# Attention with a top-32 mask and a mixer: softmax scales read in two transfers, and three edits where the first batch ends

## The chip, the cores and the metric

One core of a Trainium2 chip runs the kernel. The metric is the device time of one execution in microseconds (us); less is better. Each kernel is timed in several runs, and the median counts. One execution is also recorded by the hardware profiler: its span is the time from the first to the last recorded instruction, a little less than its device time.

## What is computed

Two blocks, one after the other, in float32 (the mixer's weights come as float64 and are converted on the chip):

```python
# attention: B=8 batches, H=8 heads, S=576 rows, D=64
scores = 1/sqrt(D) * q @ k.T
kth = np.partition(scores, -32, axis=-1)[..., -32:-31]     # the 32nd largest of each row
scores = np.where(scores >= kth, scores, -1e9)
attn = exp(scores - max(scores))
attn = attn / (sum(attn) + 1e-9)
x = (attn @ v), heads side by side                          # (8, 576, 512)
# mixer: U (576, 32), V (32, 576), w_ch1 (512, 2048), w_ch2 (2048, 512)
h = xt @ U @ V                    # along the rows; xt is x with rows and channels swapped
u = x + h.transpose(0, 2, 1)
out = u + maximum(u @ w_ch1, 0) @ w_ch2
```

## The kernel before, in words

**The unit of work** is a pair of heads, `g` from 0 to 31 (four pairs a batch, `NPAIR` = 4). A pair's 576 rows are cut into four tiles of 128 and a tail of 64 (`NT` = 4; tile 4 is the tail, in which the two heads share the partitions). The rows are dealt out so that tile t holds every fourth row. A step is one tile: in the first batch each pair has five steps; from pair 4 on the fourth tile and the tail are one step, so four steps a pair. `ALONE` = 20 is the number of the first batch's steps, 132 the number of all. Steps 20 to 23 are pair 4's, step 24 is tile 0 of pair 5, which the text writes (5,0).

**What a step does.** `scores` (L336) multiplies on PE into PSUM, and ACT copies to SBUF (L381; tail L401, L404). `front` (L454) finds each row's 32nd largest value on DVE: MAX8 gives the eight largest, MATCH_REPLACE8 takes them out, four rounds in all (L502, L515, L520). From pair 5 on (`blocked`) a row of 576 is first folded to 288: `fold` adds the two halves' bits on POOL (L432), `split` takes the larger of each two on DVE, out of PSUM (L434), and the smaller by subtraction on POOL (L435); the search then goes over the 288 larger ones and the best 16 of the smaller ones (L487, L485). The larger half lives in a buffer `upper`, of which there are two. A row that isn't folded needs a buffer `place` to take the search's first replacement; before the change that is a tile out of the same `upper` buffers, or `tplace` for the tail when three rows are searched together. After the search ACT scales the threshold (L546) and makes the mask's gap (L549), POOL subtracts it (L550), and ACT's exp (L439) adds each row's sum into a column of `den`, nine columns a pair (four tiles of two heads, and the tail).

**What follows a step.** The weights are turned for the product with v. From pair 6 on tiles 0 to 3 go by DVE's block transpose (`blocks`, L576), four DMA writes to DRAM (`away`, SP's queue, L582) and one read back (`PT`, ACT's queue, L591); tails and pairs 4 and 5 go by PE (`turns`, L612, L617) with ACT copies (L613, L618), pair 4's and later tails into the buffer `PTt`. `values` multiplies with v (L688, L691; tail L662) into XT (ACT L700, L669).

**The sums.** In the first batch `den` is applied where rows lie on partitions (L733). From pair 4 on `inverse` takes the reciprocal (DVE L629), turns it (L631), and writes nine rows of 128 to a DRAM tile `rd` in four DMAs (SP's queue, L635). One step later `scale` (L639) reads them back on ACT's queue, spread over the partitions: head 0's four rows to partitions 0 to 63, head 1's to 64 to 127, and the tail's likewise, four DMAs a pair in all (L645, L649), for 28 pairs. The rows of `rd` are in the order of `den`'s columns: before the change column 2t + c for tile t, head c.

**The mixing** (`mixed`, L703) runs in the background as a generator, a piece each time `fill` is called. From pair 4 on POOL multiplies XT by the scales (L719, L720), PE turns the result (L725, L738), and ACT copies it to a constant tile X (L729, L739). The tail's part of X has 64 rows from pair 4 on, 128 in the first batch, so its rows 64 to 127 are cleared once by a MEMSET, in pair 4's mixing (L736). Then come the products with U (`pT`, L750) and V (`up`, L762; in the first batch with L766, which adds X itself), copied and added on ACT and POOL (L775, L777, L778).

**The channel mixer** of a finished batch (`mlp`, L801: products L810 and L828, ACT L823 and L839, POOL L840) is cut into single products, which `fill` puts between the attention's instructions on PE, so many per step as a share of the work prescribes. The last batch's (`closing`, L889) runs at the end. The weights are converted by `next_params` (L218), one set at a time through a short pipeline: a raw load on SP's queue (L154), three ACT passes (L176, L177, L180), DVE L188, POOL L189 and L191.

**The order** on every engine's queue is the order in which the main loop (L1182 to L1321) issues things; nothing reorders it. A step n is: the end of the last step's exp; `weighted`, `scores` and `fold` of the next tile; `turn` and `back`; `scale` (L1287); a round of the search (`next(here)`); `next_params(1)` (L1289); a round; `split` of the next tile (L1300); the last round; `blocks` and `inverse` of the last step's tile; loads of a coming pair; `next_params(1)` when t is not 0 (L1318); the end of the search. One tile is special: the `split` of (5,0), in step 23, comes after the last round (`bound`, L1297 to L1305), because the three searches of that step hold both `upper` buffers as their places until then.

Of the kernel before, what the change touches and what calls it, by code (L numbers as in the profile page):

```python
# [26 lines left out]
def kernel(  # L27
# [30 lines left out]
    P = 128  # L58
# [78 lines left out]
    def half(h):  # L137
        return slice(h * D, (h + 1) * D)
# [79 lines left out]
    def next_params(n):  # L218

        while passes:  # L220
            passes.pop(0)()
        while parts:
            f64_join(*parts.pop(0))
        while raws:
            r, outs = raws.pop(0)
            if isinstance(outs, list):
                parts.append((*f64_parts(r, None), outs))
                continue
            hi, bits, low = f64_parts(r, outs)
            parts.append((hi, bits, low, [(bits, same)]))  # L230
        for _ in range(min(n, len(params))):
            srcs, outs = params.pop()
            raws.append((f64_raw(srcs), outs))
# [220 lines left out]
    def front(tiles):  # L454

        lanes = []
        for g, t in tiles:  # L460
            if t == 0:
                dens[g] = small.tile([P, 2 * NT + 1], F32, tag="den", name="den", bufs=3)
            S2, den = S2s.pop((g, t)), dens[g]
            early, pooled, gaps = ways(g, t)
            n = S2.shape[1]
            fold_of = folds.pop((g, t), None)
            for c in (1, 0) if n == 2 else (0,):
                slot = c if n == 2 or len(tiles) == 1 else 2
                lanes.append((
                    slot,  # L470
                    S2[:, c],
                    den[:, 2 * t + c : 2 * t + c + 1],
                    [a[:, c] for a in fold_of] if fold_of else None,
                    "early" if c in early else "pooled" if c in pooled else "gap" if c in gaps else "",
                ))
        W = len(lanes)
        first = small.tile([P, 3, 8], F32, tag="first", name="first", bufs=3)
        nmax = small.tile([P, 3], F32, tag="nmax", name="nmax", bufs=4)
        curs, places, ms = {}, {}, {}
        halves = [(lane[0], *lane[3]) for lane in lanes if lane[3]]  # L480
        for at_, step in ((0, 0), (0, 1), (8, 0)):
            for slot, upper, lower in halves:
                spot = upper[:, HALF + at_ : HALF + at_ + 8]
                if step:
                    nc.vector.match_replace(lower, spot, lower, NEG)  # L485
                else:
                    nc.vector.max(spot, lower)  # L487
        for slot, chunk, _, fold_of, _ in lanes:
            if fold_of:
                curs[slot] = fold_of[0]  # L490
            else:
                curs[slot] = chunk
                if slot == 2:
                    places[slot] = attn.tile([P, S], F32, tag="tplace", name="place", bufs=1)
                else:
                    places[slot] = attn.tile(
                        [P, 2, HALF + TOPK // 2], F32, tag="upper", name="upper"
                    ).rearrange("p c n -> p (c n)")[:, 0:S]
            ms[slot] = first[:, slot]
        order = [lane[0] for lane in lanes]  # L500
        for c in order:
            nc.vector.max(ms[c], curs[c])  # L502
        yield
        for i in range(1, TOPK // 8):
            if i == 1:
                nc.scalar.mul(nmax[:, 0:W], first[:, 0:W, 0], -SCALE)
                Es = {}
                for c, chunk, _, _, way in lanes:
                    if way == "early":
                        Es[c] = attn.tile([P, S], F32, tag="E", name="E")  # L510
                        weigh(chunk, Es[c], nmax[:, c : c + 1])
            for c in order:

                nxt = places.pop(c, curs[c])
                nc.vector.match_replace(nxt, ms[c], curs[c], NEG)  # L515
                curs[c] = nxt
            m8 = small.tile([P, 3, 8], F32, tag="m8", name="m8", bufs=4)
            for c in order:
                ms[c] = m8[:, c]
                nc.vector.max(ms[c], curs[c])  # L520
            yield
        for c, chunk, total, _, way in lanes:
            if way == "pooled":
                gap = attn.tile([P, S], F32, tag="E", name="E")
                nc.gpsimd.tensor_scalar(gap, chunk, ms[c][:, 7:8], NEG, ALU.is_lt, ALU.mult)
                nc.gpsimd.tensor_tensor(chunk, chunk, gap, ALU.add)  # L526
        for c, chunk, total, _, way in lanes:
            if way == "early":
                nc.vector.scalar_tensor_tensor(
                    out=chunk,  # L530
                    in0=chunk,
                    scalar=ms[c][:, 7:8],
                    in1=Es[c],
                    op0=ALU.is_ge,
                    op1=ALU.mult,
                    accum_out=total,
                )
        if t == NT:
            del qkTs[g]
        yield  # L540
        gaps = [lane for lane in lanes if lane[4] == "gap"]
        if gaps:
            slots = [lane[0] for lane in gaps]
            lo, hi = min(slots), max(slots) + 1
            least = small.tile([P, 3], F32, tag="least", name="least", bufs=3)
            nc.scalar.mul(least[:, lo:hi], m8[:, lo:hi, 7], WIDEN)  # L546
            for c, chunk, *_ in gaps:
                gap = attn.tile([P, S], F32, tag="E", name="E")
                nc.scalar.activation(gap, chunk, AF.Relu, bias=least[:, c : c + 1], scale=-WIDEN)  # L549
                nc.gpsimd.tensor_tensor(chunk, chunk, gap, ALU.subtract)  # L550
            yield
        rest = [lane for lane in lanes if lane[4] != "early"]
        if len(gaps) > 1:
            c, chunk, total, *_ = rest.pop(0)
            weigh(chunk, chunk, nmax[:, c : c + 1], total)
            yield
        for c, chunk, total, *_ in rest:
            weigh(chunk, chunk, nmax[:, c : c + 1], total)
        if t == NT and g != NPAIR - 1:
            nc.scalar.activation(den, den, AF.Identity, bias=eps)  # L560
        yield
# [77 lines left out]
    def scale(g):  # L639

        rd = scales.pop(g)
        sc = attn.tile([P, S], F32, tag="scale", name="scale", bufs=1)
        scales[g] = sc
        for h in range(2):
            nc.scalar.dma_start(  # L645
                sc[half(h), 0:MAIN].rearrange("p (t n) -> p t n", t=NT),
                rd[0 : 2 * NT].rearrange("(t h) n -> h t n", h=2)[h : h + 1].to_broadcast([D, NT, P]),
            )
            nc.scalar.dma_start(  # L649
                sc[half(h), MAIN:S], rd[2 * NT : 2 * NT + 1, half(h)].to_broadcast([D, TAIL])  # L650
            )

    def values(g, t):

# [48 lines left out]
    def mixed(g, wait, lag=0):  # L703
# [26 lines left out]
        if g < NPAIR:  # L730
            X4 = X4.rearrange("p t (h d) -> p t h d", h=2)
            den4 = den[:, 0 : 2 * NT].rearrange("p (t h) -> p t h ()", h=2)
            nc.gpsimd.tensor_tensor(X4, X4, den4.to_broadcast([P, NT, 2, D]), ALU.mult)  # L733
        else:
            if g == NPAIR:
                nc.gpsimd.memset(X[TAIL:P, NT, :], 0.0)  # L736
            tp = ps_t.tile([P, P], F32, tag="tp", name="tp")
            nc.tensor.transpose(tp[0:TAIL], uT[:, at(NT)], ident)  # L738
            nc.scalar.copy(X[0:TAIL, NT, :], tp[0:TAIL])  # L739
# [20 lines left out]
        for chunks, (lo, hi) in zip(PARTS, SPAN):  # L760
# [15 lines left out]
            else:  # L776
                nc.scalar.copy(sc[:, lo:hi], up[:, 0 : hi - lo])  # L777
                nc.gpsimd.tensor_tensor(uT[:, lo:hi], uT[:, lo:hi], sc[:, lo:hi], ALU.add)  # L778
            yield
        if gi == NPAIR - 1:  # L780
            fillers.append(closing(b) if b == B - 1 else mlp(b))

# [370 lines left out]
    def tiles(n):  # L1153

        return steps[n] if 0 <= n < STEPS else []
# [26 lines left out]
    for n in range(STEPS + 2):  # L1182
# [103 lines left out]
        if n < STEPS and n - 2 >= ALONE and len(tiles(n - 2)) > 1:  # L1286
            scale(steps[n - 2][0][0])  # L1287
        next(here, None)
        next_params(1)  # L1289
        fill()  # L1290
        if n >= STEPS:
            if n == STEPS:
# [1 line left out]
                scale(NP - 1)  # L1294
            weighted(n - 2)
        next(here, None)
        bound = tiles(n + 1)[:1] == [(NPAIR + 1, 0)]  # L1297
        if not bound:
            for tile_ in tiles(n + 1):
                split(*tile_)  # L1300
        fill()
        next(here, None)
        if bound:
            for tile_ in tiles(n + 1):
                split(*tile_)  # L1305
        for tile_ in tiles(n - 1):
            if shared(*tile_):
                blocks(*tile_)
# [5 lines left out]
                coming = loading(g + 2) if g + 2 < NP else iter(())  # L1314
            next(coming, None)
        next(ready, None)
        if t != 0:
            next_params(1)  # L1318
        next(here, None)
        fill()  # L1320
# [36 lines left out]
```

## Time and profile before

| | |
|---|---|
| median of 3 runs | 1684.32 us (1682.92 to 1688.65) |
| the profiled execution | 1686.09 us, span 1684.0 us |
| mean granted clock of TensorE | 0.963 |
| busy, share of the span | PE 93%, DVE 92%, ACT 59%, POOL 59% |
| DMA packets | 295631, 189.42 MB, mean 112 GB/s |
| reads of the scales | 56 of 128 KB (L645) and 56 of 16 KB (L649), on ACT's queue |

PE is TensorE (PEld its weight loads, which lie beside the products), DVE VectorE, ACT ScalarE, POOL GpSimd, SP SyncE. "ACTq" and "SPq" are an engine's issuing of DMAs. L12 is line 12 of the kernel. In a list of waits each row says which engine and line waited for which, then how long in sum, how often, and the longest. In a timeline a row is the start, the duration, the engine, the line and the operation with its shape, and in brackets how long the engine had been idle before it and who released it. The granted clock is the share of TensorE's full speed that the chip's throttle allowed.

### The profile page before, as it was taken

The numbers are of one execution on the slowest core, as the hardware profiler recorded it, in microseconds if no ns is written. First come the engines' busy times: TensorE is split into PE (matmuls) and PEld (weight loads), VectorE is DVE, ScalarE is ACT, GpSimd is POOL, SyncE is SP. The second block draws the span as 40 slices with busy tenths as digits, with TensorE's granted clock in tenths as the row PEclk, the third lists the DMA queues.
The fourth block names the chain that finished last, engine by engine and source line by source line (L and its number), as shares of the span: only waits on it lengthen the run. The fifth ranks groups of instructions, "written<-read, shape, count | busy, mean of one in ns | idle before, by whom it ended". The sixth has DMA issues, their size and how long they took to land.

```text
span 1684.0 us, 30301 instructions
## 1 busy us (share of the span) xinstructions
PE 1569.8 (93%) x9638; PEld 1189.6 (71%) x9638; DVE 1546.0 (92%) x4393; ACT 992.5 (59%) x2475; POOL 1000.3 (59%) x853
## 2 busy tenths in 40 slices
PE   4667798999899999999999999999999999999999
PEld 2444466777577886778777787778777787778776
DVE  7999998899999999999999999999999999995452
ACT  4888777665655656556655566556655566564320
POOL 4778668666656565655656565655656565653620
PEclk7787798999999999999999999999999999999999
DMA  3323232254555555555455555554555555543001
GB/s 87 96 74 96 61 94 73 56 128 130 136 128 131 134 151 131 127 138 131 124 128 139 127 139 135 132 139 124 133 128 132 133 140 136 132 126 109 10 1 29
DMA packets 295631, 189.42 MB, mean 112 GB/s; under 512 B 178768, under 2 KB 279984, under 8 KB 295472
## 3 DMA queue, kind: packets, MB, share of 16 engines
q1 hardware_dynamic: 259728, 117.62, 30.2%
q10 hardware_dynamic: 35744, 69.88, 13.6%
q8 instruction: 76, 1.25, 0.3%
q14 instruction: 83, 0.68, 0.1%
HBM read 116.49 MB, written 70.91 MB: 111 GB/s over the span
## 4 chain that ended last, share of the span: by engine, by line
DVE 47%; PE 33%; DMA 8%; SPq 4%; issue 3%; ACT 2%; POOL 1%; ACTq 0%; DVEq 0%; POOLq 0%
DVE m L520 13%; DVE upper L515 11%; PE mm L828 9%; PE mm L810 8%; DVE y L576 5%; DVE first L502 4%; DVE upper L487 4%; DMA ld<-in_k_dram 3%; PE sc L336 3%; DVE place L515 3%; PE mm L904 3%; DVE lower L485 3%; PE O L691 2%; DMA PT<-away 2%; PE sc L904 2%
## 5 line engine op out<-in xcount | busy, mean ns | idle before, releaser
L810 PE MATMUL mm<-uT,w 128*128 128x320 f32 (+1 forms) x1792 | 468.1, 413 | 14.5 <-ACT hT L823 14.1
L550 POOL TENSOR_TENSOR Ssb<-Ssb,E 128x576 f32<-128x576 f32 x243 | 340.0, 1419 | 208.8 <-ACT E L549 208.4
L828 PE MATMUL mm<-hT,w 128*128 128x320 f32 (+1 forms) x1792 | 462.8, 408 | 0.0
L810 PEld LDWEIGHTS mm<-uT,w 128*128 128x128 f32 x1792 | 336.1, 192 | 120.2 <-ACT hT L823 23.3
L828 PEld LDWEIGHTS mm<-hT,w 128*128 128x128 f32 x1792 | 332.5, 190 | 93.6 <-issue 11.0
L520 DVE MAX8 m<-upper 128x8 f32<-128x304 f32 (+1 forms) x780 | 377.8, 539 | 0.7
L515 DVE MATCH_REPLACE8 upper<-m,upper 128x304 f32<-128x304 f32 (+1 forms) x520 | 266.8, 534 | 0.0
L435 POOL TENSOR_TENSOR lower<-lower,upper 128x576 uint32<-128x576 uint32 x108 | 152.9, 1416 | 162.0 <-DVE upper L434 161.7
L439 ACT ACTIVATE Ssb<-Ssb,nmax 128x576 f32<-128x576 f32 x258 | 201.8, 783 | 32.9 <-POOL Ssb L526 9.9
L432 POOL TENSOR_TENSOR lower<-Ssb 128x576 uint32<-128x576 uint32 x108 | 152.4, 1411 | 93.3 <-ACT Ssb L381 48.7
L487 DVE MAX8 upper<-lower 128x8 f32<-128x288 f32 x432 | 176.8, 461 | 15.9 <-POOL lower L435 15.8
L336 PE MATMUL sc<-qkT 64*128 64x288 f32 (+1 forms) x1056 | 179.6, 462 | 11.0 <-ACT Ssb L390 7.8
L549 ACT ACTIVATE E<-Ssb,least 128x576 f32<-128x576 f32 x243 | 176.3, 769 | 4.2
L381 ACT COPY Ssb<-sc 128x576 f32<-128x576 f32 x216 | 127.8, 644 | 61.6 <-PE sc L336 61.6
L576 DVE STREAM_TRANSPOSE y<-Ssb 128x512 f32<-128x512 f32 (+1 forms) x312 | 157.7, 581 | 0.3 <-ACT Ssb L439 0.2
L823 ACT ACTIVATE hT<-mm 128x320 f32<-128x320 f32 (+1 forms) x224 | 91.3, 410 | 102.7 <-PE mm L810 97.9
L691 PE MATMUL O<-PT,va 128*64 128x128 f32 x2048 | 144.5, 285 | 0.0
L336 PEld LDWEIGHTS sc<-qkT 64*128 64x128 f32 (+1 forms) x1056 | 96.0, 197 | 52.0 <-issue 17.4
L691 PEld LDWEIGHTS O<-PT,va 128*64 128x64 f32 x2048 | 113.3, 140 | 16.4 <-issue 2.0
L515 DVE MATCH_REPLACE8 upper<-first,upper 128x304 f32<-128x304 f32 x216 | 100.4, 487 | 0.0
L485 DVE MATCH_REPLACE8 lower<-upper,lower 128x288 f32<-128x288 f32 x216 | 96.3, 465 | 0.0
L434 DVE TENSOR_TENSOR upper<-sc,Ssb 128x576 f32<-128x576 f32 x108 | 83.3, 772 | 11.5 <-ACT Stail L401 11.5
(264 smaller groups left out, 2246.9 us busy)
## 6 DMA issues: line engine op xcount, KB each, us to landing
away<-y SPq DMA_DIRECT2D x416, 144.0 KB
PT<-away ACTq DMA_DIRECT2D x104, 576.0 KB
raw<-in_moe_w_ch_dram SPq DMA_DIRECT2D x32, 512.0 KB
va<-in_v_dram SPq DMA_DIRECT2D x64, 128.0 KB
out_dram<-ob SPq DMA_DIRECT2D x59, 128.0 KB
scale<-rd ACTq DMA_DIRECT2D x56, 128.0 KB
ld<-in_q_dram SPq DMA_DIRECT2D x108, 64.0 KB
ld<-in_k_dram SPq DMA_DIRECT2D x108, 64.0 KB
```

The source lines that it names most:

```text
L336: nc.tensor.matmul(out, lhsT=qkT[half(h), 0, cols(t)], rhs=qkT[half(h), 1, lo:hi], start=True, stop=True,)
L435: nc.gpsimd.tensor_tensor(bottom, bottom, top.bitcast(U32), ALU.subtract)
L439: nc.scalar.activation(E, chunk, AF.Exp, bias=nmax, scale=SCALE, accum_out=total)
L487: nc.vector.max(spot, lower)
L515: nc.vector.match_replace(nxt, ms[c], curs[c], NEG)
L520: nc.vector.max(ms[c], curs[c])
L549: nc.scalar.activation(gap, chunk, AF.Relu, bias=least[:, c : c + 1], scale=-WIDEN)
L550: nc.gpsimd.tensor_tensor(chunk, chunk, gap, ALU.subtract)
L576: nc.vector.transpose(y[:, :, i * NT : i * NT + c].rearrange("p r c j -> p c r j"), E2[:, a : a + c * P].rearrange("p (c r j) -> p c r j", ...
L691: nc.tensor.matmul(O[half(h)], lhsT=va[:, h, j, :], rhs=PT[:, NT * h + j], start=False, stop=(j == NT - 1),)
L810: nc.tensor.matmul(ph[:, 0:w], lhsT=first_layer(cc, f), rhs=uT[:, cc, lo:hi], start=(cc == 0), stop=(cc == NC - 1),)
L828: nc.tensor.matmul(po[:, 0:w], lhsT=w2[:, f, c * P : (c + 1) * P], rhs=hTs[f][:, 0:w], start=(f == 0), stop=(f == NF - 1),)
```

## The change

Four edits.

1. *Scales.* From pair 4 on the columns of `den` are ordered by head: column 4c + t. The scale rows of one head are then 2 KB in a row in DRAM, and `scale` reads all 128 partitions' main part in one DMA (source 2 heads, each repeated for 64 partitions, 512 values) and the tail's in another (2 x 64 repeats x 64 values). Two DMAs a pair in the place of four, on the same queue at the same place.
2. *The sixth pair's first fold.* The searches of step 23 take their places from the `scale` and `PTt` buffers, which hold nothing yet, so the `split` of (5,0) comes where that of every other tile does, ahead of the last round.
3. *Parameters.* Step 23 leaves out its first `next_params(1)`; step 24 gets one at its end. From step 25 on as many have been done as before.
4. *X's rows.* The MEMSET of rows 64 to 127 moves from pair 4's mixing to the end of pair 3's.

```diff
@@ front
             for c in (1, 0) if n == 2 else (0,):
                 slot = c if n == 2 or len(tiles) == 1 else 2
+                spot = NT * c + t if g >= NPAIR and t < NT else 2 * t + c
                 lanes.append((
                     slot,
                     S2[:, c],
-                    den[:, 2 * t + c : 2 * t + c + 1],
+                    den[:, spot : spot + 1],
...
                 if slot == 2:
                     places[slot] = attn.tile([P, S], F32, tag="tplace", name="place", bufs=1)
+                elif (g, t) == (NPAIR, NT):
+                    places[slot] = attn.tile([P, S], F32, tag="scale", name="place", bufs=1) if slot else (
+                        attn.tile([P, NT + 1, P], F32, tag="PTt", name="place", bufs=1)
+                    ).rearrange("p c n -> p (c n)")[:, 0:S]
                 else:
@@ scale
-        for h in range(2):
-            nc.scalar.dma_start(
-                sc[half(h), 0:MAIN].rearrange("p (t n) -> p t n", t=NT),
-                rd[0 : 2 * NT].rearrange("(t h) n -> h t n", h=2)[h : h + 1].to_broadcast([D, NT, P]),
-            )
-            nc.scalar.dma_start(
-                sc[half(h), MAIN:S], rd[2 * NT : 2 * NT + 1, half(h)].to_broadcast([D, TAIL])
-            )
+        full = rd[0 : 2 * NT].rearrange("(h t) n -> h () (t n)", h=2)
+        nc.scalar.dma_start(sc[:, 0:MAIN], full.to_broadcast([2, D, MAIN]))
+        ends = rd[2 * NT : 2 * NT + 1].rearrange("o (h n) -> (o h) () n", h=2)
+        nc.scalar.dma_start(sc[:, MAIN:S], ends.to_broadcast([2, D, TAIL]))
@@ mixed
-            if g == NPAIR:
-                nc.gpsimd.memset(X[TAIL:P, NT, :], 0.0)
...
+        if g == NPAIR - 1:
+            nc.gpsimd.memset(X[TAIL:P, NT, :], 0.0)
         if gi == NPAIR - 1:
             fillers.append(closing(b) if b == B - 1 else mlp(b))
@@ the main loop
         next(here, None)
-        next_params(1)
+        border = g == NPAIR and t == NT - 1
+        if not border:
+            next_params(1)
         fill()
...
-        bound = tiles(n + 1)[:1] == [(NPAIR + 1, 0)]
-        if not bound:
-            for tile_ in tiles(n + 1):
-                split(*tile_)
+        for tile_ in tiles(n + 1):
+            split(*tile_)
         fill()
         next(here, None)
-        if bound:
-            for tile_ in tiles(n + 1):
-                split(*tile_)
...
-        if t != 0:
+        if t != 0 or g == NPAIR + 1:
             next_params(1)
```

## The prediction, made before the result was known

> **What bounds the kernel now.** I read the page first (busy shares, chain by engine), then the windows table by stage, then the waits of the long stage, then the timelines around the places that the change touches.
>
> ```profile
> PE 1569.8 (93%) x9638; PEld 1189.6 (71%) x9638; DVE 1546.0 (92%) x4393; ACT 992.5 (59%) x2475; POOL 1000.3 (59%) x853
> DVE 47%; PE 33%; DMA 8%; SPq 4%; issue 3%; ACT 2%; POOL 1%; ACTq 0%; DVEq 0%; POOLq 0%
> ```
>
> Two engines share the end: DVE's search and TensorE's products. The table by stage (start and end, length, then busy time of PE, PEld, DVE, ACT, POOL, granted clock, DMA share, GB/s) says where each has room:
>
> ```profile
> 240.00:330.00 90.00, 81.13 (x455) 57.59 (x454) 76.10 (x227) 62.04 (x143) 64.92 (x53) 0.91 0.22 57
> 330.00:1530.00 1200.00, 1178.14 (x7523) 905.16 (x7522) 1179.33 (x3579) 712.53 (x1806) 721.63 (x610) 0.99 0.53 132
> 1530.00:1684.00 154.00, 148.31 (x699) 118.09 (x698) 61.61 (x109) 35.02 (x90) 48.21 (x58) 0.99 0.12 29
> ```
>
> In the 90 us in which the kernel goes over from the first batch to the rest (the border), PE is idle 8.9 us and DVE 13.9. In the long stage each is idle some 21 us of 1200. So a gain must be found in about 22 us of the long stage and 9 to 14 of the border, and it needs both engines: one alone would stop at the other. In the last 154 us DVE is half empty and PE nearly full, so what comes a little late there costs nothing.
>
> What ends DVE's idle time in the long stage is almost all of two kinds (waits of that window: us, times, longest):
>
> ```profile
> DVE upper L434 <- ACT Stail L401: 11.5, 6, 3.5
> DVE upper L487 <- POOL lower L435: 8.1, 5, 2.4
> ```
>
> The timelines lead both back to the reads of the scales. ACT at 934, with its queue's issues:
>
> ```profile
> 934.68 0.62 ACTq L645 DMA_DIRECT2D scale<-rd  x1
> 935.34 0.63 ACTq L649 DMA_DIRECT2D scale<-rd  x1
> 935.99 0.62 ACTq L645 DMA_DIRECT2D scale<-rd  x1
> 939.07 0.47 ACTq L649 DMA_DIRECT2D scale<-rd  x1
> 939.59 0.20 ACT L506 ACTIVATE nmax<-first 128x2 f32<-128x2 f32 x1 [4.26 <-DMA ld<-in_k_dram]
> ```
>
> The fourth read is not issued until 939.07. By the trace's semaphore records the DMAs of both queues raise eight semaphores in turn, and a DMA waits until the one eight before it has landed; here that is a load of keys issued a microsecond before the scales. ACT is in order, so hT (L823), oT (L839) and the copies of scores queue behind it. Around 990 the same hold comes through ACT and POOL to DVE:
>
> ```profile
> 990.44 0.73 POOL L840 TENSOR_TENSOR oT<-oT,uT 128x256 f32<-128x256 f32 x1 [5.65 <-ACT oT L839]
> 991.13 1.42 POOL L435 TENSOR_TENSOR lower<-lower,upper 128x576 uint32<-128x576 uint32 x1
> 992.58 0.82 DVE L487 MAX8 upper<-lower 128x8 f32<-128x288 f32 x2 [2.33 <-POOL lower L435]
> ```
>
> Call s the start of a pair's first scale read. From s to the end of the fourth ACT is held 2.6 to 5.0 us, mean 3.75 over 28 pairs. All ten DVE stalls over 0.5 us of the long stage (17.5 us in sum) follow such a hold; of PE's gaps, 8.8 us do.
>
> **Scales in two reads, 28 pairs.** Four issues go (medians 622 and 626 ns by the lines' own view), two come. Their price is not in the trace in this form; issues of other forms take 0.33 us (PT, L591) to 0.65 (the reads themselves), so two cost 0.65 to 1.3; I take 1.24, the form replaced. The third and fourth issue and the fourth's wait go, so the hold falls from 3.75 to 1.24, 2.5 us in each pair. If nothing comes late for it, DVE gets back up to 17.5 us. PE gets 8.8, and half of one half-clock window of 3.4 us that follows such a gap (941.2 to 944.6), 1.7: 10.5. Both must run ahead together, so I take 12, between them.
>
> Against it stands the landing. The old reads land 4.45 us (L645) and 3.68 (L649) after issue, all by s+6, and POOL first needs the scales (L719) at s+10.4 to s+12.5. The new main read fills 128 rows of 2 KB out of a source whose outer dimension is 2. How far it spreads over the DMA engines is not shown. Nearly every DMA of the trace has an outer dimension of 32 to 128 and raises its semaphore 16 times; the one with 9 rows (rd<-rows) raises it 10 times. So the count seems to follow the outer dimension, and I take two engines, the value nearest to that row. Packets of 512 B take 27 ns, of 4608 B 178 ns; 2 KB lies at about 84 by interpolation (an estimate). On two engines that is 64 x 84 ns = 5.4 us, and the tails' 64 x 18 ns = 1.15 behind it; with some 2.3 us to the first completion and PT's read (L591) in front on the same queue, the main read lands at s+8 at best, s+10.7 as I take it, s+12.3 if `away` writes share those engines all along. On 16 engines it would be 8 x 84 ns = 0.7 us, landing near s+4.
>
> The spread of L719, s+10.4 to s+12.5, is itself the hold's; with a short hold it wants to start near s+10.4 in every pair. A landing at s+10.7 then makes it 0.3 us late, and PE's transposes L725 follow L720 by only 0.1 to 0.7: 28 x 0.3 = 8 us given back on PE. DVE has 0.8 to 2.6 us to spare behind POOL there. The eight semaphores turn too: with two DMAs fewer, the next PT<-away (ACT, due at s+9 to s+10) waits for the tails' read in about 7 of 25 pairs, some 2.2 us each, 15 us of ACT hold; of the old 36.7 us of such waits 17.5 reached DVE, so of these about 7 do. What is queued behind is what was behind the fourth read: hT, oT, least. In about 12 pairs the fourth away write (SP, s+7 to s+8) waits for the main read, and PT after it. PE and DVE losses lie beside each other: 8 in all. Net of the reads: 12 - 8 = 4 us gained; bounds: 17.5 gained (16 engines, nothing late) and, at s+12.3, 28 x 1.9 = 53 given back against 12.
>
> The Trainium skill, "DMA: Bandwidth & Descriptors", section "Why a DMA increments its semaphore by 16 and not by 1", speaks against this edit: the number of engines comes from the slowest dimension that isn't 1, of both sides, and a leading broadcast dimension of 2 keeps the whole transfer on two engines. The rows of the replaced reads, 16 increments each, would by themselves say 16. By the rule the reads bring the 4 us above; by those rows alone 12 to 17.
>
> **The border.** Four edits act between 245 and 340.
>
> First, (5,0)'s split (DVE L434, POOL L435) goes back ahead of the last search round, since the search no longer borrows the `upper` buffers. Now PE and DVE both wait for it:
>
> ```profile
> 248.62 1.33 PE L336 MATMUL sc<-qkT 64*128 64x288 f32 x4 [2.18 <-DVE upper L434]
> 250.20 0.82 DVE L487 MAX8 upper<-lower 128x8 f32<-128x288 f32 x2 [1.30 <-POOL lower L435]
> ```
>
> L434 moves past six search instructions (about 4.5 us) on DVE; POOL, idle 6.3 us there, takes L435 under them. 2.18 us of PE and 1.30 of DVE go. The borrowed `scale` and `PTt` buffers are first used a step later (PTt at 270.2, scale at 271.5), and their first users only write after the search is over: nothing waits.
>
> Second, one parameter set (DVE L188 0.4 to 0.9 us, POOL L189 and L191 2.6, ACT 2.2, one raw load on SP) leaves this step and comes back at the end of the next; the count after that is the same. POOL has 2.56 us idle at 262.6 to 265.2, which covers 2.57; without that cover (5,1)'s fold L432 comes 2.6 us later. I count it at nothing. Late next is the reciprocal L629, 2.19 us behind ACT L560, which stays.
>
> Third, the shorter first hold of ACT (271.5 to 274.4) lets L176 go earlier: DVE's 3.06 us at L188 (275.26) falls to about 1.
>
> Fourth, the MEMSET of X. PE waits for it behind POOL's parameter work, and then runs at half clock:
>
> ```profile
> 293.13 0.63 PE L750 MATMUL pT<-x,U 128*32 128x128 f32 x2 [2.54 <-POOL x L736]
> 292.70:299.50 6.80, 6.37 (x20) 3.96 (x21) 6.80 (x20) 2.56 (x5) 5.36 (x6) 0.50 0.00 0
> ```
>
> In the fourth pair's mixing it waits for PE's L766 (end at 209.8), and POOL is idle from 209.9 to 214.0, so its 0.2 us is free; behind it stands L550, which waits for ACT until 214.0 anyway. Gone are 2.54 us of PE and half of 6.8 at half clock, 3.4; and with them the DVE stalls that follow, 3.5 us at L487 (306.8) and perhaps 2.1 at L434 (335.7).
>
> Sum for PE: 2.18 + 2.54 + 3.4 = 8.1. For DVE: 1.3 + 2 + 3.5 + half of 2.1 = 7.9. I take 8; bounds 3 (the memset's own gap, if another wait comes into the rest) and 13 (PE's 3.66 us at 256.1 and DVE's other stalls go too).
>
> **Sum.** Border 8 + reads 4 = 12 us. The profiled execution took 1686.09 (span 1684.0 and 2.1 around it), 1.77 above the median of the runs; 1686.1 - 12 = 1674.1 there, 1672 for the median.
>
> **The rivals.**
> A, *the late landing takes the gain back*. For it: L725 stands 0.1 to 0.7 us behind POOL, nothing to spare. At 0.6 us in each pair, 17 us go; 8 + 12 - 17 = 3 gained: about 1681.
> B, *slower: both reads crowd on two DMA engines*. Its place is POOL's L719, with PE's L725 behind it: the main read lands at s+11.5, L719 waits 1.1 us in each of 28 pairs, 31 us, against 8 + 12 of gains: +11, about 1695; at the end of the bounds, s+12.3, 53 - 20 = +33, 1717. It decides from a landing of s+11.1 on (0.7 us x 28 = 20). For it: the `away` writes, which run at s+3 to s+8 over the same engines; against it: PE's fillers and DVE's slack can take part of a late L719.
> C, *the reads spread as before*. They land by s+4 to s+5, nothing is late, 12 to 17 from the reads and 8 or more from the border: about 1662, down to 1655.
> That an edit does not do what it says: if the border's gaps are only refilled by other waits, its bound of 3 with 0 from the reads gives 1681 too, part of A.
>
> **Numbers.** Forecast (1666 to 1678) 0.46, A 0.18, B 0.24, C 0.12. A run tells 0.3%, 5 us, from no change. Faster: forecast and C and a little of A, 0.60; same: the rest of A, 0.16; slower: B, 0.24. Range 1656 to 1698, which leaves out the lower part of C (0.04) and B beyond its middle (0.11); the forecast's own range is 1666 to 1678.
>
> **What the profile after would show.** The reads: 28 + 28 issues, the ACT idle behind k loads (L506) gone; semaphores of the new reads raised 2 or 3 times (two engines) or 16; a wait of POOL L719 for the scales, or of PE L725 for L719, larger than now if they come late; PT's issue waiting longer if the lanes hit. The border: no PE wait at L750 for the MEMSET, no half clock at 293, no L336 wait for L434. I am wrong if DVE's stalls at L434 and L487 stay with a short hold (then ACT's hold was not their cause), or if L719 starts past s+11.

## The result: slower by 0.6%

The changed kernel takes 1697.03 us (median of 6 runs, 1695.49 to 1699.01) against 1686.51 (6 runs, 1682.92 to 1689.25): ratio 1.0063, 95% interval 1.0048 to 1.0079. The forecast, 12 us faster, was wrong in its sign. The range, 1656 to 1698, holds the time, and the slower rival B named 1695, but, as will be seen, at the wrong place.

### The profile after

The page's busy shares and its chain (the changed kernel's line numbers are the same up to L439 and mostly one to five higher behind it; L487 is L488, the reads are L650 and L652, `away` is L587, PT L596, the multiplication by the scales L720; every run below has its own line numbers):

```profile
PE 1565.0 (92%) x9638; PEld 1181.5 (70%) x9638; DVE 1548.5 (91%) x4393; ACT 992.7 (59%) x2475; POOL 999.6 (59%) x853
DVE 53%; DMA 25%; PE 10%; SPq 6%; issue 2%; ACT 2%; ACTq 1%; POOL 0%; DVEq 0%; POOLq 0%
DVE m L525 14%; DMA scale<-rd 13%; DVE upper L520 12%; DMA ld<-in_k_dram 6%; DVE y L581 5%; DVE upper L488 5%; DVE first L507 5%; DVE place L520 4%; DVE lower L486 3%; DMA ld<-in_q_dram 3%; PE mm L905 3%; SPq L258 2%; DVE qkT L306 2%; PE sc L905 2%; PE tp L905 2%
```

The engines' work is within 5 us of before, but transfers are now a quarter of the chain (8% before), and half of that is the scale reads. The table by stage, columns as before:

```profile
240.00:330.00 90.00, 83.24 (x525) 59.97 (x524) 82.23 (x241) 64.53 (x152) 68.35 (x54) 0.96 0.26 65
330.00:1530.00 1200.00, 1166.29 (x7414) 891.00 (x7414) 1168.78 (x3543) 706.56 (x1785) 714.09 (x605) 1.00 0.52 131
```

The border became denser (DVE 82.2 of 90 us, 76.1 before; clock 0.96, 0.91 before). The long stage lost 12 us of PE's busy time and 11 of DVE's in the same 1200 us. DVE's waits there, and PE's longest:

```profile
DVE qkT L306 <- DMA ld<-in_k_dram: 29.7, 17, 3.2
DVE y L581 <- ACT Ssb L439: 0.6, 1, 0.6
```

```profile
PE O L689 <- DMA PT<-away: 11.9, 17, 1.8
PE mm L811 <- ACT hT L824: 11.5, 14, 1.4
```

The old stalls at L434 and L487 are gone from this stage to the last one. In their place DVE waits 29.7 us for loads of keys, which it turns at L306 for the next pair. Since L306 stands once in each pair, its start, counted from the span's start, marks how far a kernel has come. Changed minus before, in us, from the two traces, at the L306 of pair

| 6 | 7 | 9 | 12 | 16 | 20 | 24 | 28 | 31 | end |
|---|---|---|---|---|---|---|---|---|---|
| -0.8 | -6.6 | -5.0 | -2.5 | +3.0 | +2.0 | +3.0 | +4.8 | +7.3 | +10.5 |

The border brings about 6.6 us, the long stage takes 13.9, the end from the last keys on 3.2 more.

### How a scale read reaches DVE

One pair in the changed kernel; the ACT queue at s = 938.68:

```profile
938.68 0.51 ACTq L650 DMA_DIRECT2D scale<-rd  x1
939.23 0.52 ACTq L652 DMA_DIRECT2D scale<-rd  x1
```

The hold of ACT is over after 1.06 us. Then SP's queue and DVE:

```profile
944.28 4.24 SPq L587 DMA_DIRECT2D away<-y  x4
950.08 0.59 SPq L258 DMA_DIRECT2D ld<-in_k_dram  x1
950.72 0.63 SPq L263 DMA_DIRECT2D ld<-in_k_dram  x1
951.39 0.58 SPq L258 DMA_DIRECT2D ld<-in_k_dram  x1
952.02 0.62 SPq L263 DMA_DIRECT2D ld<-in_k_dram  x1
```

```profile
955.74 1.38 DVE L306 STREAM_TRANSPOSE qkT<-ld 128x1152 f32<-128x1152 f32 x1 [1.47 <-DMA ld<-in_k_dram]
```

The trace's landings fill in the rest. The main read lands at s+9.5 and the tails' at s+11.4 (950.1). The four `away` writes take 4.24 us to issue where 1.8 is usual. The third waits until 946.8 for the semaphore of a load of keys, which was issued 0.2 us behind the main read and took 7.9 us to land; the fourth waits until 948.2 for the semaphore that the main read holds. The next load of keys waits for the tails' semaphore and goes out at 950.08, the moment that it is free. Three more loads stand behind it, they land together at about 955.5, and DVE has been waiting since 954.3. Over the long stage SP waits 39 times for a semaphore that a scale read holds, 53.6 us in sum (the time from the end of its last issue to the next, where that one goes out within 0.8 us of the landing); in the kernel before it is never. Another 14 times, 21.3 us in sum, the third or fourth `away` write waits for the semaphore of a load of keys that lands late: 34 of the stage's 192 loads of keys take over 7 us to land, and none does before (the longest takes 6.0). So the two reads stop SP's queue by their own semaphores, and by those of the loads that land late beside them.

Each of the two reads raises its semaphore 3 times, where each of the four of before raised it 16 times; as in the prediction, this is read as two engines. They land 9.2 and 10.6 us after their issue (medians; before 4.45 and 3.68).

### The profile page after: what moved, and what is told of

Read it like the earlier page. It is cut to its first block, busy times and chain, and to the rows that moved or that the text cites. A ratio compares the mean times of both kernels' runs of the same rounds, so it can differ in the third digit from the quotient of the medians.

```text
span 1694.5 us, 30176 instructions
## 1 busy us (share of the span) xinstructions
PE 1565.0 (92%) x9638; PEld 1181.5 (70%) x9638; DVE 1548.5 (91%) x4393; ACT 992.7 (59%) x2475; POOL 999.6 (59%) x853
## 3 DMA queue, kind: packets, MB, share of 16 engines
q10 hardware_dynamic: 23312, 69.87, 12.8%
## 4 chain that ended last, share of the span: by engine, by line
DVE 53%; DMA 25%; PE 10%; SPq 6%; issue 2%; ACT 2%; ACTq 1%; POOL 0%; DVEq 0%; POOLq 0%
DVE m L525 14%; DMA scale<-rd 13%; DVE upper L520 12%; DMA ld<-in_k_dram 6%; DVE y L581 5%; DVE upper L488 5%; DVE first L507 5%; DVE place L520 4%; DVE lower L486 3%; DMA ld<-in_q_dram 3%; PE mm L905 3%; SPq L258 2%; DVE qkT L306 2%; PE sc L905 2%; PE tp L905 2%
## 5 line engine op out<-in xcount | busy, mean ns | idle before, releaser
L525 DVE MAX8 m<-upper 128x8 f32<-128x304 f32 (+1 forms) x774 | 362.9, 510 | 0.7
L520 DVE MATCH_REPLACE8 upper<-m,upper 128x304 f32<-128x304 f32 (+1 forms) x516 | 256.8, 505 | 0.0
L439 ACT ACTIVATE Ssb<-Ssb,nmax 128x576 f32<-128x576 f32 x258 | 201.8, 782 | 42.7 <-DMA away<-y 14.4
L488 DVE MAX8 upper<-lower 128x8 f32<-128x288 f32 x432 | 172.0, 439 | 1.4 <-POOL lower L435 1.3
L581 DVE STREAM_TRANSPOSE y<-Ssb 128x512 f32<-128x512 f32 (+1 forms) x312 | 154.1, 545 | 0.6 <-ACT Ssb L439 0.6
L551 ACT ACTIVATE least<-m 128x2 f32<-128x2 f32 (+2 forms) x131 | 26.7, 204 | 128.9 <-DVE m L525 128.7
```

The source lines that it names most:

```text
L439: nc.scalar.activation(E, chunk, AF.Exp, bias=nmax, scale=SCALE, accum_out=total)
L581: nc.vector.transpose(y[:, :, i * NT : i * NT + c].rearrange("p r c j -> p c r j"), E2[:, a : a + c * P].rearrange("p (c r j) -> p c r j", ...
```

## The experiments

Theory 1: the two reads lie on two DMA engines, land late, and hold semaphores for which SP's queue waits, so that keys come late. Theory 2: with two DMAs fewer the semaphores turn differently against SP's queue, however fast the reads are. Theory 3: the border's edits cost, the reads do not. Each ratio is to the kernel before, run on the same chip in turn with it. The kernel before had a median of 1683.88 to 1686.51 us from one round to the next, so compare the ratios rather than the medians.

| kernel | median us | ratio, 95% interval | mean hold of ACT | main read lands |
|---|---|---|---|---|
| the change | 1697.03 | 1.0063, 1.0048 to 1.0079 | 1.1 | 9.2 |
| reads_only | 1696.69 | 1.0079, 1.0054 to 1.0104 | 1.1 | 9.2 |
| border_only | 1678.77 | 0.9970, 0.9954 to 0.9986 | 3.7 | 4.4 |
| four_engines | 1666.49 | 0.9898, 0.9871 to 0.9925 | 1.1 | 6.4 |
| three_reads | 1661.71 | 0.9868, 0.9842 to 0.9894 | 1.7 | 4.5 |
| four_long | 1679.27 | 0.9968, 0.9948 to 0.9988 | 3.7 | 4.4 |
| memset_only | 1680.50 | 0.9973, 0.9953 to 0.9993 | 3.8 | 4.4 |
| fold_param_only | 1681.36 | 0.9974, 0.9956 to 0.9992 | 3.8 | 4.4 |
| three_old_border | 1665.77 | 0.9881, 0.9854 to 0.9909 | 1.7 | 4.5 |
| keys_sooner | 1710.44 | 1.0139, 1.0117 to 1.0161 | 1.1 | 9.0 |
| three_keys_sooner | 1662.05 | 0.9859, 0.9843 to 0.9876 | 1.7 | 4.6 |

(Hold: from the first scale issue to the end of the last, us, mean over pairs 5 to 30; landing: median from a main read's own issue, us.)

**The parts alone.** border_only is the change with the four reads and the old columns:

> The change without its two reads: four reads a pair and the old order of the sums; the three edits at the border stay. Theory 1 (both reads on two DMA engines land 9 to 11 us after s, SP's queue waits for their semaphores, the keys come late for DVE L306): the border's 7 us stay and nothing else, 1679.5 us against 1686.5. Theory 2 (two DMAs fewer turn the eight semaphores against SP's queue, however fast the reads are): the same, 1679.5. Theory 3 (the border edits cost, the reads do not): 1695 or more.

reads_only is the kernel before with the new columns and

```diff
-        for h in range(2):
-            nc.scalar.dma_start(
-                sc[half(h), 0:MAIN].rearrange("p (t n) -> p t n", t=NT),
-                rd[0 : 2 * NT].rearrange("(t h) n -> h t n", h=2)[h : h + 1].to_broadcast([D, NT, P]),
-            )
-            nc.scalar.dma_start(
-                sc[half(h), MAIN:S], rd[2 * NT : 2 * NT + 1, half(h)].to_broadcast([D, TAIL])
-            )
+        full = rd[0 : 2 * NT].rearrange("(h t) n -> h () (t n)", h=2)
+        nc.scalar.dma_start(sc[:, 0:MAIN], full.to_broadcast([2, D, MAIN]))
+        ends = rd[2 * NT : 2 * NT + 1].rearrange("o (h n) -> (o h) () n", h=2)
+        nc.scalar.dma_start(sc[:, MAIN:S], ends.to_broadcast([2, D, TAIL]))
```

> The kernel before with the two reads and the new order of the sums, without the three border edits. Theories 1 and 2: 1686.5 + 13.9 (long stage) + 3.2 (tail), as the traces of before and after differ, about 1703 us, with some 30 us of DVE L306 waits for loads of keys. Theory 3: 1680 to 1687.

Theory 3 falls: the border's edits bring 0.3% and the reads cost 0.8% (1696.69 us, where theories 1 and 2 gave about 1703), with the waits for keys that these two named:

```profile
DVE qkT L306 <- DMA ld<-in_k_dram: 25.4, 16, 2.8
```

Whether the two parts add up can't be told from the times: 0.8% less 0.3% is 0.5%, the change has 0.6%, and the intervals are wider than the difference. In the two traces the border's head start melts (3.7 us at pair 7, 1.5 at pair 20, none at pair 24). Why was not found out.

**More engines.** three_reads gives each head a read of its own, so that the outer dimension is 64:

```diff
-        full = rd[0 : 2 * NT].rearrange("(h t) n -> h () (t n)", h=2)
-        nc.scalar.dma_start(sc[:, 0:MAIN], full.to_broadcast([2, D, MAIN]))
+        for h in range(2):
+            nc.scalar.dma_start(
+                sc[half(h), 0:MAIN],
+                rd[0 : 2 * NT].rearrange("(h t) n -> h (t n)", h=2)[h : h + 1].to_broadcast([D, MAIN]),
+            )
```

> The change, but the main read is two DMAs, one for each head, 64 rows of 2 KB, so that its outer dimension is 64; the tails stay one DMA with outer dimension 2. Theory 1: the main reads land by s+6, the tails by s+7 (64 x 18 ns on two engines); L306's wait for keys falls from 30 us to under 8 and the old ACT hold is mostly gone: 1668 to 1680 us. Theory 2 (rotation alone, one DMA fewer than before): 1688 to 1697, L306 waits stay above 15 us.

four_engines keeps the change's two DMAs, and doubles each head's rows in DRAM:

```diff
-        nc.vector.reciprocal(upright[:, 0 : 2 * NT + 1], den)
+        twice = upright[:, 0 : 4 * NT].rearrange("p (h j t) -> p h j t", h=2, j=2)
+        mains = den[:, 0 : 2 * NT].rearrange("p (h t) -> p h () t", h=2)
+        nc.vector.reciprocal(twice, mains.to_broadcast([P, 2, 2, NT]))
+        nc.vector.reciprocal(upright[:, 4 * NT : 4 * NT + 1], den[:, 2 * NT :])
...
-        full = rd[0 : 2 * NT].rearrange("(h t) n -> h () (t n)", h=2)
-        nc.scalar.dma_start(sc[:, 0:MAIN], full.to_broadcast([2, D, MAIN]))
+        full = rd[0 : 4 * NT].rearrange("(h t) n -> h () (t n)", h=4)
+        nc.scalar.dma_start(sc[:, 0:MAIN], full.to_broadcast([4, BLK, MAIN]))
...
```

(The parts left out make the DRAM tile 18 rows high, write all 18, and take the tail's rows from their new place.)

> The change with each head's four rows written twice to DRAM (18 rows in the place of 9), so that the one main read has an outer dimension of 4 and each part carries 32 rows of 2 KB; the number and order of DMAs is that of the change. Theory 1: semaphores raised 5 times, the main read lands at about s+6.5 to s+7.5, L306 waits fall below 15 us, 1674 to 1688 us. Theory 2: the rotation is that of the change, so 1695 to 1699 us and 30 us of L306 waits.

Theory 2 falls with four_engines. Its DMAs are those of the change in number and order, and on each queue every one has the semaphore that it has in the change; but the main read raises its semaphore 5 times (4 engines) and lands at 6.4 us in the place of 9.2, and the kernel is 1.6% faster than the change (0.9898 against 1.0063). DVE's waits in its long stage:

```profile
DVE upright L636 <- ACT den L565: 6.4, 1, 6.4
DVE qkT L306 <- DMA ld<-in_k_dram: 1.2, 1, 1.2
```

One wait for keys is left of 17 (the other is the last pair's reciprocal; before, the same 6.4 us stand at 1540.7, beyond this window). The time was below the range that theory 1 gave, 1674 to 1688: I had thought the short hold worth less. So too three_reads, 1661.7 where 1668 was the lower end. Its SP queue at the same place of a pair (s = 921.48) shows what is not there any more:

```profile
926.83 1.77 SPq L587 DMA_DIRECT2D away<-y  x4
928.65 0.59 SPq L258 DMA_DIRECT2D ld<-in_k_dram  x1
```

The four writes go out in 1.77 us, the keys right behind. The last keys of a pair are issued at s+9.0 and land at s+11.6 on average (changed kernel s+12.1 and s+15.5), and L306 does not wait.

**Hold or packets.** four_long has three_reads' long rows, but a tail read for each head again, four reads in all in the old order (the diff is to three_reads):

```diff
         for h in range(2):
             nc.scalar.dma_start(
                 sc[half(h), 0:MAIN],
                 rd[0 : 2 * NT].rearrange("(h t) n -> h (t n)", h=2)[h : h + 1].to_broadcast([D, MAIN]),
             )
+            nc.scalar.dma_start(
+                sc[half(h), MAIN:S], rd[2 * NT : 2 * NT + 1, half(h)].to_broadcast([D, TAIL])
+            )
-        ends = rd[2 * NT : 2 * NT + 1].rearrange("o (h n) -> (o h) () n", h=2)
-        nc.scalar.dma_start(sc[:, MAIN:S], ends.to_broadcast([2, D, TAIL]))
```

> The change with four reads a pair again, in the old order of issue, but each head's main read as 64 rows of 2 KB in the place of 64 x 4 of 512 B. Theory 1a (what three reads gain over four is ACT's hold: the fourth read's wait for a semaphore): the hold stays near 3.7 us, DVE's stalls at L434 and L487 stay, 1676 to 1681 us, as border_only. Theory 1b (the gain is the longer rows: fewer packets, a lighter DMA load): 1660 to 1668 us.

It is border_only again, with its hold (3.7 us) and its two old kinds of stall:

```profile
DVE upper L434 <- ACT Stail L401: 10.7, 4, 3.6
DVE upper L488 <- POOL lower L435: 7.9, 6, 2.4
```

With one read fewer, in three_reads, they are gone. The gain is the hold's, not that of longer rows.

**The border's edits apart.** memset_only moves only X's clearing, fold_param_only has the other two edits:

> The kernel before with only the MEMSET of X moved to the fourth pair's mixing. If the prediction's border sum is right: PE's 2.5 us before L750 and the half clock after it go, with DVE's 3.5 us at L487 behind them, so 4 to 6 us less than before, 1678 to 1682 where before is 1684 to 1686. If another wait takes their place: within 2 us of before.

> The kernel before with only the fold of (5,0) at its usual place (places in the scale and PTt buffers) and one parameter set moved from step 23 to the end of step 24. By the prediction's border sum 2 to 3 us less than before, 1681 to 1684; if the parameter set costs at its new place what it saves, no difference.

Each brings 0.3%, and both together bring 0.3% (border_only); that looks like less than their sum, but the three intervals are too wide to show it. In memset_only the half clock at 293 is gone (0.50 before), and the clock of 240 to 330 rises from 0.91 to 0.96:

```profile
240.00:330.00 90.00, 80.71 (x518) 58.24 (x517) 80.02 (x239) 62.32 (x148) 66.96 (x53) 0.96 0.25 64
292.70:299.50 6.80, 6.80 (x32) 4.99 (x31) 6.80 (x18) 3.50 (x11) 6.72 (x7) 1.00 0.07 20
```

three_old_border is the three reads without the border:

> The kernel before with the three reads alone, without the border's edits. If reads and border add up: 1661.7 + 5 (what border_only gained) = 1667 us. If the border's gain is absorbed later, as with the two reads (the change 1697.0, reads_only 1696.7): 1662 us.

The median lies nearer to adding up (1667) than to absorbing (1662); but by the ratios the border brings only 2 us here (0.9881 against 0.9868), with intervals that overlap, so this stays open.

**Keys out of the way.** keys_sooner is the whole change, with the second half of the key loads a step sooner (and the loads of v that follow them):

```diff
                 if i:
                     yield
                 for a in range(4):
-                    if i and a == 2:
-                        yield
```

> The change, two-engine reads and all, but the second half of a pair's key loads is issued a step sooner, with the first half, ahead of the scale reads in SP's queue (and the loads of v a step sooner). If the late keys at L306 are what the two reads cost (30 us of waits): L306's waits fall under 8 us and the time to 1665 to 1680 us, though the reads still land at s+9 to s+11 on two engines. If the cost lies in crowded engines and late PT or away transfers in general: the waits move to PE's PT (L688) or DVE elsewhere and the time stays at 1690 to 1697.

> The change with one main read for each head and the same sooner loads of keys. Keys are not waited for at L306 with three reads (no such wait in three_reads), so by the theory of late keys nothing is gained: 1659 to 1665 us.

This refuted the narrow form of theory 1, that late keys are the price. No L306 wait is left, and the kernel is slower still, outside the ranges of both expectations. DVE's waits now, and PE's longest:

```profile
DVE y L579 <- DMA away<-y: 22.4, 21, 3.0
DVE y L579 <- ACT Ssb L437: 17.1, 24, 0.9
PE O L687 <- DMA PT<-away: 14.0, 16, 2.8
```

With the keys gone from behind the reads, the `away` writes stand there: SP waits 36 times in an `away` issue for a scale read's semaphore, 58 us in sum (10 times and 13.6 us in the change). `y` has one buffer, so DVE cannot turn the next tile until they are out. (What makes DVE wait for L437 was not followed; in three_keys_sooner that wait is 0.3 us.) The keys now run beside the scale reads and land 6.0 us after issue (3.63 before, 4.55 in the change), yet DVE never waits for them. So the price of the two reads is SP's queue, held until they and the transfers beside them land, and whatever is next in it pays (here the `away` writes, and PE's wait for PT with them, 14.0 us). three_keys_sooner, where the reads land early, is three_reads again, as expected; its loads of keys, issued at the same place, land in 3.6 us.

How much of the late keys is the reads' own semaphores and how much the crowding of two engines is told apart only by the traces: in the change the last load of keys is issued 2.6 us later than before (s+12.1 against s+9.5) and lands 0.9 us more slowly (3.4 against 2.5). The 2.6 us hold crowding too, since 21.3 us of SP's waits are for loads of keys that were slow themselves. No run has the one without the other.

## Why the prediction was wrong, point by point

- *What bounds the kernel; ACT's hold as the cause of the stalls*: right. The hold fell to 1.1 us (1.24 predicted), and every stall of the long stage at L434 and L487 went (reads_only keeps one, 2.1 us). Its worth was under-sized: three_reads against border_only, 17.1 us, at the top of the bounds 10.5 to 17.5 from which I took 12; there PE's wait for hT in the long stage falls from 12.8 to 2.8 us.
- *Two engines*: right, from the row with 9 rows and 10 increments. Outer dimensions of 2, 4 and 64 gave 3, 5 and 16 increments. By the Trainium skill ("DMA: Bandwidth & Descriptors", "Why a DMA increments its semaphore by 16 and not by 1") each engine that a DMA uses raises the semaphore once, the issuing sequencer adds what is missing to 16 at once, and the number of engines is the largest up to 16 that divides the slowest dimension of both sides; every count here agrees, as one record for each engine and one for the sequencer's addition. The packets of 2 KB took 84 ns (median), as interpolated. The landing, s+10.7 predicted, is s+9.3 for the main read, and s+11.2 for the tails.
- *L719 late, 8 us on PE*: wrong. In the numbers of before: the multiplication L719 starts at s+10.9 on average and the tails' L720 at s+12.3; L719 never waits for the scales, and L720 in two pairs, by 0.4 and 0.7 us. My sign of being wrong, a start of L719 past s+11, came in 9 of the long stage's 25 pairs (14 before), each time with the scales already there.
- *The step that failed* is the next one: "In about 12 pairs the fourth away write (SP, s+7 to s+8) waits for the main read, and PT after it", summed up in "PE and DVE losses lie beside each other: 8 in all". I looked at which DMA takes the semaphore, followed ACT's queue behind it, and did not follow SP's: behind that write stand four loads of keys, and L306 behind them. The write waits for the main read in 10 pairs, 13.6 us. The loads themselves wait for the reads' semaphores 29 times, 40 us, and `away` writes 14 times, 21.3 us, for loads of keys that land late; for both the sum had no term at all. In the place of the 8 us given back stand some 33: reads_only against three_old_border, which differ in the main read alone (one DMA or two), 1.0079 - 0.9881 = 0.0198 of 1685 us.
- *The border, 8 us*: measured 5 (0.30%, 0.14 to 0.46), 6.6 in the traces at pair 7. The memset's part is right, the half clock included. Of the fold's, PE's 2.18 us did not go: it went over to the next wait, as the line of the changed kernel shows (3.66 before); only DVE gained. The parameter set had its cover: (5,1)'s fold starts at 268.2, 268.4 before. DVE's wait at L188 fell to 2.2 us only, not to 1, and the stall at L434 at the end of the border stayed (1.9 us, 2.1 before).

```profile
254.46 1.12 PE L617 MATMUL tp<-ident,Ssb 128*128 128x128 f32 x4 [6.14 <-ACT XT L701]
```

- *The sum* of the measured terms: border -5, hold -17, the queue behind the reads +33, together +11; measured +10.6 (0.63% of 1685). Each term is known only to some 3 to 6 us, so part of this agreement is luck.
- *Rival B* had the sign, the crowding and nearly the time, but placed it at L719, which never waited. *Rival C* is what three_reads shows: 1661.7, where C said 1662.
- *The end ("what comes a little late there costs nothing")*: not borne out; from the last keys to the end the change needs 3.2 us more. three_reads, whose reads land early, needs 2.4 more as well, so it isn't the reads' landing alone; without the border's edits it is 5.0 (reads_only) and 0.1 (three_old_border). The cause stays open.

## What to carry to other kernels

A DMA is paid for in four places: its issue, its landing, the engines that carry it, and the semaphore that it holds until it lands; the last stops whichever queue comes round to it, with all that is queued behind. When transfers are merged, keep the outer dimension wide, as far as this case shows: two reads with an outer dimension of 2 lost 0.8% by themselves, and three, the main ones with 64, won 1.2%. Where a prediction finds a queue that will wait, follow that queue's next instructions to their readers before giving the wait a price.

## What the runs showed that I had not expected

The main read of 256 KB landed after 9.2 us on 2 engines, 6.4 on 4, and 4.5 as two reads on 16: eight times the engines halve the time. If the time is a fixed part and one that goes with the number of engines, the step from 2 to 4, 2.8 us, makes 5.6 us of streaming on two engines (the estimate was 5.4 from packet times) and leaves 3.6 us that are there in any form; this is an estimate from two points. Crowding showed too: in keys_sooner the loads of keys beside a two-engine read took 6.0 us to land, against 3.6 in three_keys_sooner, where the reads land early.
